# Gated units over batches [0], [1,2], [3,4], [5,6], [7], weights converted in their order of use, exponentials without bias operand, norm of pooled queries

## The chip, the core and the metric

The kernel runs on one core of a Trainium2 chip. The metric is the device time of one execution in microseconds (us). The core's engines run their own instruction queues, each in order: TensorE (PE in the profile; its weight loads are PEld) multiplies matrices, VectorE (DVE), ScalarE (ACT) and GpSimd (POOL) work element by element, and SyncE (SP) issues the DMA transfers.

## The reference, cut to what matters

```python
def _attn_ref(q, k, v):                       # B, H, S, D = 8, 8, 1152, 64
    q_pool = q.reshape(B, H, S // 2, 2, D).mean(axis=3)
    scores = 1 / np.sqrt(D) * np.matmul(q_pool, k.transpose(0, 1, 3, 2))
    scores = scores - np.max(scores, axis=-1, keepdims=True)
    attn = np.exp(scores)
    attn = attn / (np.sum(attn, axis=-1, keepdims=True) + 1e-09)
    return np.matmul(attn, v)                 # 576 rows a head

def _moe_ref(x, w_in, w_spatial, b_spatial, w_out):   # x: 8 x 576 x 512
    h = np.maximum(x @ w_in, 0.0)                     # w_in: 512 x 1024
    u, v = h[..., :512], h[..., 512:]
    v_n = (v - mean(v)) / np.sqrt(var(v) + 1e-06)     # over the last axis
    v_s = np.einsum('ts,bsd->btd', w_spatial, v_n) + b_spatial[None, :, None]
    return (u * v_s) @ w_out                          # w_out: 512 x 512
```

The attention's output, heads side by side, is the second function's x. `w_in` and `w_out` arrive as 64-bit floats.

## The kernel before

Every matrix product is made of products of 16-bit halves: a number is split into a head (ScalarE, `head`) and a rest (VectorE, `rest`), after a scaling by a power of two that is found from the sum of squares (`square_sum` on ScalarE, then `scales`: a matmul with ones and three small VectorE operations).

**Attention** goes over 32 pairs; pair i holds two heads of one batch, four pairs make a batch (`NHP = 4`). While pair i's scores, exponentials and products with v are made (`attention(i)`, 40 steps), generators beside it are stepped at fixed rates (`Pace`): the row maxima of pair i+1 (`maxima`, 27 matmuls, each followed by a VectorE maximum over 384 columns), the loading and splitting of v (`values_ahead`), and the preparation of pair i+2's queries and keys (`prep`). `prep` squares and sums keys and both halves of the queries, then adds the halves (the pooling) on GpSimd. A score tile of 128 x 512 goes through PSUM tile `pss` (three buffers) into an exponential on ScalarE (`main_tile`), with `lnp`, a constant column of log 64, as bias and `esc`, the pair's scale, as scale. GpSimd splits the result (`split`, tile `pt`), and TensorE multiplies it with v into `o`. The maxima go into the scores as two more rows of the contraction, stored in `xq`.

**Gated units.** The second function runs in units of two batches (`gated_unit`), four in all. A unit makes 9 tiles of v (L582), their mean and variance, an inverse square root of 16 small operations on VectorE (L611 to L614), u in 12 pieces (L646) with `normalise` of one v tile after each of the first nine, 8 spatial products with the gate (L688, L689), `split(0)` of the product, and 9 output tiles (L731). While pairs run, the unit in front of the list `units` gets 0.5 of its steps per attention step (`MOE_RATE`); what is left at the end is drained. The last unit splits its product in two groups, so that a spatial product stands between them.

**Weights** are converted on the way: `load_weights` takes `w_in` in 8 pieces and `w_out` in 4, two staging tiles in turn (the next piece's transfer is issued before the present one is used), 0.25 steps per attention step (`W_RATE`), done by the end of pair 7; then `load_spatial` is stepped from within the first unit's v tiles. `from_double` makes a 32-bit float from two integer words.

The program order so written is then rearranged, engine by engine, when the program is built: an instruction can move ahead of others that aren't ready. Each engine keeps the built order on the chip.

Of the kernel before, what the change touches and what calls it, by code (L numbers as in the profile page):

```python
# [13 lines left out]
I32 = mybir.dt.int32  # L14
I64 = mybir.dt.int64
AF = mybir.ActivationFunctionType
# [15 lines left out]
def attn_sgu_kernel(ctx: ExitStack, tc: tile.TileContext, qT, kT, v, w_in, w_spT, b_sp, w_out, out):  # L32
# [18 lines left out]
    NU = B // 2  # L51
    WS_STEPS = 2
    MOE_RATE = 0.5
    D1 = D + 1
    VW = 2 * D + 2

# [18 lines left out]
    lnp = const.tile([P, 1], F32, name="lnp")  # L75
    nc.vector.memset(lnp, math.log(PEXP))
# [67 lines left out]
    def from_double(dst, src, t1, t2):  # L144
# [3 lines left out]
        lo, hi = src[:, 0::2], src[:, 1::2]  # L148
        V.tensor_scalar(out=t1, in0=hi, scalar1=0xFFFFF, scalar2=None, op0=ALU.bitwise_and)
        nc.scalar.activation(dst, t1, AF.Copy, bias=1.0, scale=2.0 ** -20)  # L150
        V.tensor_scalar(out=t2, in0=lo, scalar1=1, scalar2=None, op0=ALU.logical_shift_right)
        yield
        V.scalar_tensor_tensor(out=dst, in0=t2, scalar=2.0 ** -51, in1=dst, op0=ALU.mult, op1=ALU.add)
# [12 lines left out]
    def load_weights():  # L166
        for name, w, wh, wl, n, m in (("wi", w_in, wi_h, wi_l, NCC, DF), ("wo", w_out, wo_h, wo_l, NFC, DM)):
            f32 = mo.tile([P, NT * DH], F32, name="u")
            raw = mo.tile([P, NT * DH], F32, name="vv")

            st = [raw[:, j * 1024 : (j + 1) * 1024].bitcast(I32) for j in range(2)]
            t1, t2 = (raw[:, 2048 + j * 512 : 2560 + j * 512].bitcast(I32) for j in range(2))
            jk = raw[:, 3072 : 3072 + 512]
            pieces = [(c, a) for c in range(n) for a in range(0, m, 512)]
            sq = const.tile([P, len(pieces)], F32, name=name + "q")

            def fetch(j):
                c, a = pieces[j]
                nc.sync.dma_start(out=st[j % 2].bitcast(I64), in_=w[c * P : (c + 1) * P, a : a + 512])

            fetch(0)
            for j, (c, a) in enumerate(pieces):
                if j + 1 < len(pieces):
                    fetch(j + 1)
                d = f32[:, c * m + a : c * m + a + 512]
                yield from from_double(d, st[j % 2], t1, t2)
                square_sum(sq[:, j : j + 1], d, jk)
            s, wsc[name] = yield from scale_of(sq, name)
            yield
            for c, a in pieces:  # L190
                d = f32[:, c * m + a : c * m + a + 512]
                head(wh[:, c, a : a + 512], d, s)
                rest(wl[:, c, a : a + 512], d, s, wh[:, c, a : a + 512])
                yield

    def load_spatial():
        f32 = mo.tile([P, NT * DH], F32, name="u")
        sq = const.tile([P, 5], F32, name="wsq")
        w5 = f32[:, : 5 * S].rearrange("p (c s) -> p c s", s=S)
        nc.sync.dma_start(out=w5[:, 0:4, :], in_=w_spT[0:MAIN, :].rearrange("(c p) s -> p c s", p=P))  # L200
        for half in range(2):
            nc.sync.dma_start(out=w5[half * TAIL : (half + 1) * TAIL, 4, :], in_=w_spT[MAIN:S, :])
        nc.sync.dma_start(out=b_bc, in_=b_sp.rearrange("(o s) -> o s", o=1).broadcast_to([P, S]))
        yield
        for c in range(5):
            square_sum(sq[:, c : c + 1], w5[:, c, :], ws_l[:, c, :])
            yield
        s, wsc["ws"] = yield from scale_of(sq, "ws")
        yield
        for c in range(5):  # L210
            head(ws_h[:, c, :], w5[:, c, :], s)
            rest(ws_l[:, c, :], w5[:, c, :], s, ws_h[:, c, :])
            yield

# [58 lines left out]
    def prep(i):  # L273
# [6 lines left out]

        sq = sm.tile([P, 2], F32, name="sq", bufs=2)
        for j in range(2):
            square_sum(sq[:, j : j + 1], kq[:, j * KEYS : (j + 1) * KEYS], KL[:, 0].rearrange("p c k -> p (c k)"))
            yield
# [5 lines left out]
        st["esc"] = esc  # L290
        s_k, s_q = s[:, 0:1], s[:, 1:2]
        nc.gpsimd.tensor_add(q0, q0, q1)
# [24 lines left out]
    def maxima(i):  # L317
# [34 lines left out]
        nc.vector.reduce_max(out=mx, in_=mt, axis=AX.X)  # L352
        yield
# [23 lines left out]
    W_RATE = 0.25  # L377
    W_AT = 4
    MAX_RATE = 1.0

    units = []

    def unit_step():
        if step(units[0]) is None:
            units.pop(0)
# [3 lines left out]
    def ends_unit(i):  # L389
        return i % (2 * NHP) == 2 * NHP - 1  # L390
# [59 lines left out]
    def turn_main(i):  # L450

        b, hp = divmod(i, NHP)
        n, e = divmod(b, 2)
# [6 lines left out]
        if hp == NHP - 1:  # L460
# [5 lines left out]
            if ends_unit(i):  # L466
                units.append(gated_unit(n))
# [30 lines left out]
    def attention(i):  # L498
# [10 lines left out]
        def main_tile(pt, c, h):  # L509
            ps = ps_s.tile([P, MAIN], F32, name="pss")  # L510
            products(ps, c, h, MAINS[h])
            nc.scalar.activation(pt, ps, AF.Exp, bias=lnp, scale=esc)  # L512

        def tail_tile(h, n):
# [5 lines left out]
            nc.scalar.activation(ptl[:, a:z, h], o, AF.Exp, bias=lnp, scale=esc)  # L520
# [25 lines left out]
    def gated_unit(un):  # L546
        b0, b1 = 2 * un, 2 * un + 1

        tiles = [(j * P, [(b0, j * P, 0, P)]) for j in range(4)]
        tiles.append((MAIN, [(b0, MAIN, 0, TAIL), (b1, MAIN, TAIL, P)]))  # L550
        tiles += [(MAIN + P + j * P, [(b1, j * P, 0, P)]) for j in range(4)]
        pieces = ((0, MAIN), (MAIN, MAIN + P), (MAIN + P, S2))
        last = un == NU - 1
        turn = [0]

        def bank():
# [9 lines left out]
        r_h = sm.tile([P, 3], F32, name="r_h")  # L566
# [269 lines left out]
    for g in units:  # L836
        drain(g)
# [45 lines left out]
```

## Time and profile before

| | |
|---|---|
| median of 3 runs | 1370.36 us (1369.91 to 1372.92) |
| profiled execution | 1378.83 us, span 1377.1 us, mean granted TensorE clock 0.967 |
| busy PE, PEld | 1222.1 us (89%), 741.5 us (54%) |
| busy DVE, ACT, POOL | 967.1 us (70%), 970.6 us (70%), 847.0 us (62%) |
| DMA | 123.77 MB, mean 90 GB/s |
| first exponential starts, last one | 48.5 us, 1265.7 us |

A share of busy time is a mean over stages with different limits. A busy TensorE isn't TensorE at its peak, since matmuls overlap; how many it starts in a stretch tells more. The granted clock is the share of full speed that TensorE got.

### The profile page before, as it was taken

Reading aid. Unit: us, or ns where it says so; the run is one execution under the profiler, and the core shown is the slowest. Engines: PE = TensorE matmul, PEld = TensorE weight load, DVE = VectorE, ACT = ScalarE, POOL = GpSimd, SP = SyncE. Lnnn points to the kernel's source line nnn. Section 1 sums busy time; section 2 is a strip of 40 time slices with the busy share of each in tenths; the row PEclk is TensorE's granted clock in tenths of the full one; section 3 lists DMA queues with packets and bytes.
Section 4 is the critical chain, followed back from the end, with each engine's and each line's share of the span. In section 5 each row is a group of like instructions: output and inputs, shape, how many; then the busy total and the mean of one; then the engine's idle time right before and its main releaser. Section 6 shows DMA issues by size and latency. Waiting matters only on the chain.

```text
span 1377.1 us, 33478 instructions
## 1 busy us (share of the span) xinstructions
PE 1222.1 (89%) x13696; PEld 741.5 (54%) x13696; DVE 967.1 (70%) x2068; ACT 970.6 (70%) x1632; POOL 847.0 (62%) x492
## 2 busy tenths in 40 slices
PE   3677887788998999889998999889998999899998
PEld 1354555555554665556555666555555566556443
DVE  5799889986869767765668766775667866761455
ACT  6777678779966777768776886768776776655333
POOL 3587677878755666657774766667666576655000
PEclk9998899989999999999999999999999999999999
DMA  7533343434333231244332132244331131101002
GB/s 252 166 97 109 94 124 94 128 93 139 113 96 96 79 94 56 62 126 135 96 96 87 51 91 84 74 118 135 104 96 42 47 94 55 28 24 40 8 1 69
DMA packets 56346, 123.77 MB, mean 90 GB/s; under 512 B 8256, under 2 KB 16448, under 8 KB 56192
## 3 DMA queue, kind: packets, MB, share of 16 engines
q1 hardware_dynamic: 56192, 121.63, 29.8%
q8 instruction: 107, 1.75, 0.5%
q14 instruction: 47, 0.39, 0.1%
HBM read 83.56 MB, written 9.44 MB: 68 GB/s over the span
## 4 chain that ended last, share of the span: by engine, by line
PE 47%; DVE 25%; ACT 8%; POOL 7%; DMA 7%; issue 4%; SPq 1%; POOLq 0%; ACTq 0%; DVEq 0%
DVE mt L348 7%; PE pss L507 5%; PE pss L506 5%; PE pw L688 5%; POOL pt L524 4%; PE pm L342 4%; PE pw L731 4%; PE pw L646 3%; PE o L435 3%; PE o L428 3%; PE pw L582 3%; ACT pt L512 3%; DMA kq<-in_qT_dram 3%; PE o L432 3%; DVE vv L138 2%
## 5 line engine op out<-in xcount | busy, mean ns | idle before, releaser
L524 POOL TENSOR_TENSOR pt<-pt 128x1024 f16<-128x1024 f32 x288 | 567.8, 1977 | 265.9 <-ACT pt L512 253.8
L512 ACT ACTIVATE pt<-pss,lnp,esc 128x512 f32<-128x512 f32 x576 | 439.4, 776 | 156.7 <-PE pss L507 148.1
L348 DVE TENSOR_REDUCE mt<-pm 128x1 f32<-128x384 f32 x730 | 395.8, 552 | 139.1 <-PE pm L342 119.2
L435 PE MATMUL o<-vp,pt 128*128 128x65 f16 x2304 | 282.8, 198 | 20.2 <-POOL pt L524 19.9
L428 PE MATMUL o<-vp,pt 128*128 128x65 f16 x2304 | 284.8, 196 | 13.0 <-DVE xm L443 12.8
L506 PE MATMUL pss<-qhi,khi 128*128 128x64 f16 (+1 forms) x1152 | 279.6, 294 | 9.1 <-ACT pt L512 8.0
L432 PE MATMUL o<-vp,pt 128*128 128x64 f16 x2304 | 284.5, 196 | 0.0
L507 PE MATMUL pss<-xq,klo 66*128 66x64 f16 (+1 forms) x1152 | 280.6, 295 | 4.1 <-DMA xq<-mr 4.1
L428 PEld LDWEIGHTS <-pt 128*128 128x128 bf16 x2304 | 222.7, 101 | 85.1 <-DVE xm L443 22.0
L432 PEld LDWEIGHTS <-pt 128*128 128x128 bf16 x2304 | 221.6, 100 | 50.7 <-issue 10.5
L342 PE MATMUL pm<-khi,qhi 128*128 128x384 f16 x652 | 217.9, 335 | 32.6 <-DVE mt L348 27.7
L435 PEld LDWEIGHTS <-pt 128*128 128x128 f16 x2304 | 220.7, 100 | 31.6 <-POOL pt L524 24.8
L507 PEld LDWEIGHTS <-klo 66*128 66x128 f16 x1152 | 99.1, 100 | 48.8 <-issue 17.3
L132 ACT ACTIVATE klo<-kq 128x1152 f16<-128x1152 f32 x64 | 74.6, 1166 | 63.7 <-DMA kq<-in_kT_dram 49.4
L506 PEld LDWEIGHTS <-khi 128*128 128x128 f16 x1152 | 103.5, 100 | 27.9 <-issue 12.2
L342 PEld LDWEIGHTS <-qhi 128*128 128x128 f16 x768 | 76.8, 101 | 66.3 <-issue 28.5
L524 POOL TENSOR_TENSOR ptl<-ptl 128x1152 f16<-128x1152 f32 x32 | 71.1, 2221 | 57.9 <-ACT ptl L520 57.9
L305 POOL TENSOR_TENSOR klo<-kq,khi 128x640 f16<-128x640 f32 x64 | 85.1, 1341 | 20.1 <-ACT khi L304 19.8
L520 ACT ACTIVATE ptl<-pss,lnp,esc 128x256 f32<-128x256 f32 (+1 forms) x128 | 75.6, 591 | 24.8 <-PE pss L507 24.2
L264 POOL TENSOR_TENSOR vp<-vt,vp 128x576 f16<-128x576 f32 x64 | 80.6, 1264 | 20.3 <-ACT vp L262 20.3
L582 PE MATMUL pw<-wi_h,xg 128*128 128x512 f16 x240 | 90.1, 382 | 0.0
L731 PE MATMUL pw<-wo_h,vv 128*128 128x512 f16 x216 | 80.3, 381 | 4.7 <-DVE vv L138 4.7
(177 smaller groups left out, 2394.2 us busy)
## 6 DMA issues: line engine op xcount, KB each, us to landing
vt<-in_v_dram SPq DMA_DIRECT2D x64, 576.0 KB
kq<-in_kT_dram SPq DMA_DIRECT2D x32, 576.0 KB
kq<-in_qT_dram SPq DMA_DIRECT2D x32, 576.0 KB
khi<-khi SPq DMA_DIRECT2D x96, 144.0 KB
out_dram<-row SPq DMA_DIRECT2D x24, 256.0 KB
qhi<-xq SPq DMA_DIRECT2D x64, 72.0 KB
klo<-klo SPq DMA_DIRECT2D x32, 144.0 KB
vv<-in_w_in_dram SPq DMA_DIRECT2D x8, 512.0 KB
```

The source lines that it names most:

```text
L305: nc.gpsimd.tensor_sub(KL[:, 0, a:z], k0[:, a:z], khh[:, 1, a:z])
L342: nc.tensor.matmul(pm[:, :W], lhsT=qhl[:, h, c0 : c0 + P], rhs=khh[:, h, n * NB : (n + 1) * NB, :], start=True, stop=True,)
L348: nc.vector.reduce_max(out=mt[:, t, n : n + 1], in_=pm[:, :W], axis=AX.X)
L428: nc.tensor.matmul(o[:, t], lhsT=top[:, cols], rhs=vp[:, D : D + D1], start=c == 0 and t == 0, stop=False, skip_group_check=True,)
L432: nc.tensor.matmul(o[:, t, 0:D], lhsT=top[:, cols], rhs=vp[:, 0:D], start=False, stop=False, skip_group_check=True)
L435: nc.tensor.matmul(o[:, t], lhsT=rst[:, cols], rhs=vp[:, D : D + D1], start=False, stop=c == NC - 1, skip_group_check=True,)
L506: nc.tensor.matmul(o, lhsT=khh[:, h, c, :], rhs=qhl[:, h, q], start=True, stop=False)
L507: nc.tensor.matmul(o, lhsT=KL[0:KR, h, c, :], rhs=X[0:KR, h, q], start=False, stop=True)
L512: nc.scalar.activation(pt, ps, AF.Exp, bias=lnp, scale=esc)
L524: nc.gpsimd.tensor_sub(t.bitcast(F16)[:, :, 0::2], t, t.bitcast(BF16)[:, :, 1::2])
L582: nc.tensor.matmul(ph, lhsT=xa[:, cc, c0 : c0 + P], rhs=wa[:, cc, DH:DF], start=n == 0, stop=n == 3 * NCC - 1,)
L731: nc.tensor.matmul(py, lhsT=ga[:, fc, c0 : c0 + P], rhs=wa[:, fc, :], start=m == 0, stop=m == end - 1)
```

## The change

1. Units are now batch 0 alone, then [1,2], [3,4], [5,6], then batch 7 alone: five instead of four. The first can start after four pairs instead of eight, and gets 0.36 steps per attention step; the others get 0.55. A unit of one batch has 5 tiles instead of 9 (its last tile holds 64 rows that are already in another) and makes u in 8 pieces of 288 columns.
2. Weights are converted in the order in which a unit needs them: the half of `w_in` for v, the half for u, the spatial weights, `w_out`, at 0.34 steps per attention step. There is one staging tile; the next piece's transfer is issued when the present one has been used. `need` steps the conversion to the end of a part if a unit comes early. Unit 0's tiles `u0` and `vv0` share their memory with the conversion.
3. `from_double` no longer shifts the low word: it is read as unsigned, with a stride of two words.
4. The exponentials have no bias operand. Instead `prep` makes a column `lnp` from the pair's scales (a VectorE operation and a minimum), and `maxima` subtracts it from the row maxima.
5. `prep` adds the query halves first, on GpSimd, and ScalarE squares the 576 columns of the sum instead of 1152.
6. Any unit that runs after the last score may use the score buffers `pss` (before: the last unit). Only the last unit, batch 7, has two groups.

```diff
-    NU = B // 2
-    WS_STEPS = 2
-    MOE_RATE = 0.5
+    UNITS = [(0,)] + [(b, b + 1) for b in range(1, B - 1, 2)] + [(B - 1,)]
+    NU = len(UNITS)
+    MOE_RATE = [0.36] + [0.55] * (NU - 1)
+    W_RATE = 0.34
+    W_AT = 4
...
-        lo, hi = src[:, 0::2], src[:, 1::2]
+        lo, hi = src.bitcast(U32)[:, 0::2], src[:, 1::2]
         V.tensor_scalar(out=t1, in0=hi, scalar1=0xFFFFF, scalar2=None, op0=ALU.bitwise_and)
         nc.scalar.activation(dst, t1, AF.Copy, bias=1.0, scale=2.0 ** -20)
-        V.tensor_scalar(out=t2, in0=lo, scalar1=1, scalar2=None, op0=ALU.logical_shift_right)
         yield
-        V.scalar_tensor_tensor(out=dst, in0=t2, scalar=2.0 ** -51, in1=dst, op0=ALU.mult, op1=ALU.add)
+        V.scalar_tensor_tensor(out=dst, in0=lo, scalar=2.0 ** -52, in1=dst, op0=ALU.mult, op1=ALU.add)
...
+    def load_matrix(name, w, wh, wl, a, x0):
+        st = vv0[:, V_FREE : V_FREE + 1024].bitcast(I32)
...
+        fetch(0)
+        yield
+        for c in range(n):
+            d = u0[:, x0 + c * 512 : x0 + (c + 1) * 512]
+            yield from from_double(d, st, t1, t2)
+            if c + 1 < n:
+                fetch(c + 1)
+            square_sum(sq[:, c : c + 1], d, t1.bitcast(F32))
+            yield
...
+        yield from load_matrix("wiv", w_in, wi_h, wi_l, DH, 0)
+        ready.add("wiv")
+        yield from load_matrix("wiu", w_in, wi_h, wi_l, 0, U_FREE)
+        ready.add("wiu")
+        yield from load_spatial()
+        ready.add("ws")
+        yield from load_matrix("wo", w_out, wo_h, wo_l, 0, U_FREE)
+        ready.add("wo")
+    weights = Pace(load_weights(), W_RATE, W_AT)
+    def need(name):
+        while name not in ready:
+            weights.gen = step(weights.gen)
...
+        nc.gpsimd.tensor_add(q0, q0, q1)
         sq = sm.tile([P, 2], F32, name="sq", bufs=2)
-        for j in range(2):
-            square_sum(sq[:, j : j + 1], kq[:, j * KEYS : (j + 1) * KEYS], KL[:, 0].rearrange("p c k -> p (c k)"))
-            yield
+        square_sum(sq[:, 0:1], kq[:, 0:KEYS], junk)
+        yield
+        yield
+        square_sum(sq[:, 1:2], q0, junk[:, :S])
+        yield
...
+        nc.vector.scalar_tensor_tensor(
+            out=lnp, in0=s[:, 0:1], scalar=math.log(PEXP) / ESC, in1=s[:, 1:2], op0=ALU.mult, op1=ALU.mult
+        )
+        nc.vector.tensor_scalar_min(lnp, lnp, 2.0 ** 29)
-        nc.gpsimd.tensor_add(q0, q0, q1)
...
         nc.vector.reduce_max(out=mx, in_=mt, axis=AX.X)
+        nc.vector.tensor_scalar_sub(mx, mx, st["lnp"])
...
-            nc.scalar.activation(pt, ps, AF.Exp, bias=lnp, scale=esc)
+            nc.scalar.activation(pt, ps, AF.Exp, bias=0.0, scale=esc)
...
-            if last and turn[0] % 5 > 1:
+            if not scores_left[0] and turn[0] % 5 > 1:
                 return ps_s.tile([P, MAIN], F32, name="pss")
...
+            weights.tick()
+            if units:
+                credit = min(credit + MOE_RATE[units[0][0]], 2.0)
```

Three places in the built order. First VectorE, where the conversion meets the scales of a prepared pair; before, in pair 3:

```order
L348 TENSOR_REDUCE mt<-pw 128x1 x2
L151 TENSOR_SCALAR vv<-vv 128x512
L117 TENSOR_SCALAR qkh<-pm 128x2
L153 SCALAR_TENSOR_TENSOR u<-vv,u 128x512
L348 TENSOR_REDUCE mt<-pm 128x1
L121 TENSOR_SCALAR qks<-qkh 128x2
L402 TENSOR_TENSOR xg<-pm,xg 128x512
L122 TENSOR_SCALAR qkr<-qkh 128x2
L348 TENSOR_REDUCE mt<-pm 128x1
L287 SCALAR_TENSOR_TENSOR esc<-qkr 128x1
```

and now, in pair 1 (line 413 is the maximum, 346 `esc`, 171 the conversion's first operation):

```order
L139 TENSOR_SCALAR qkh<-pm 128x2
L171 TENSOR_SCALAR vv<-vv 128x512
L413 TENSOR_REDUCE mt<-pm 128x1
L143 TENSOR_SCALAR qks<-qkh 128x2
L144 TENSOR_SCALAR qkr<-qkh 128x2
L413 TENSOR_REDUCE mt<-pw 128x1
L346 SCALAR_TENSOR_TENSOR esc<-qkr 128x1
L352 SCALAR_TENSOR_TENSOR lnp<-qks 128x1
L413 TENSOR_REDUCE mt<-pm 128x1
L355 TENSOR_SCALAR lnp<-lnp 128x1
```

The shift (151) is gone, and two operations for `lnp` stand behind `esc`.

Second, VectorE where unit 0 is normalised: before in pair 10, with the conversion of `w_in` and `w_out` over:

```order
L618 TENSOR_SCALAR row<-vv,mv,rs 128x512
L348 TENSOR_REDUCE mt<-pm 128x1
L618 TENSOR_SCALAR row<-vv,mv,rs 128x512
L402 TENSOR_TENSOR xg<-pm,xg 128x512
L624 TENSOR_TENSOR vv<-row,vv 128x512 x2
L348 TENSOR_REDUCE mt<-pm 128x1 x5
```

and now in pair 6 (703 and 709 normalise, 171 and 174 convert):

```order
L703 TENSOR_SCALAR row<-vv,mv,rs 128x512
L413 TENSOR_REDUCE mt<-pm 128x1 x2
L709 TENSOR_TENSOR vv<-row,vv 128x512
L413 TENSOR_REDUCE mt<-pm 128x1 x3
L703 TENSOR_SCALAR row<-vv,mv,rs 128x512
L171 TENSOR_SCALAR vv<-vv 128x512
L413 TENSOR_REDUCE mt<-pm 128x1 x2
L709 TENSOR_TENSOR vv<-row,vv 128x512
```

Normalising and conversion now share VectorE with the maxima.

Third, TensorE after the last score, at the matmul with ones that begins the split of a unit's product; before, in the last unit:

```order
L688 MATMUL pw<-ws_l,vv 128x512
L689 LDWEIGHTS vv
L689 MATMUL pw<-ws_l,vv 128x64
L112 MATMUL pm<-gt,ones 128x1
L688 LDWEIGHTS vv
L688 MATMUL pss<-ws_h,vv 128x512
L689 LDWEIGHTS vv
L689 MATMUL pss<-ws_h,vv 128x64
```

and now, in unit [5,6] (775 and 776 are the spatial product, 820 the output):

```order
L775 MATMUL pw<-ws_l,vv 128x512
L776 LDWEIGHTS vv
L776 MATMUL pss<-ws_l,vv 128x64
L134 MATMUL pm<-gt,ones 128x1
L820 LDWEIGHTS vv
L820 MATMUL pss<-wo_h,vv 128x512
L820 LDWEIGHTS vv
L820 MATMUL pss<-wo_l,vv 128x512
```

Where a further spatial product followed the matmul with ones, the outputs follow it now.

More of the change, by code (lines that the diff above doesn't have):

```diff
@@ L164, in attn_sgu_kernel @@
     wsc = {}
[L166 to L188, printed above, removed]
-            yield
[L190 to L193, printed above, removed]
-                yield
@@ L519, in tail_tile @@
             o = ps[:, : (z - a) * TAIL].rearrange("p (c s) -> p c s", s=TAIL)
-            nc.scalar.activation(ptl[:, a:z, h], o, AF.Exp, bias=lnp, scale=esc)
+            nc.scalar.activation(ptl[:, a:z, h], o, AF.Exp, bias=0.0, scale=esc)
         def split(t):
@@ L662, in gated_unit @@
                 yield
+        need("ws")
+        r_v = sm.tile([P, 1], F32, name="r_v")
+        nc.vector.tensor_scalar_mul(r_v, wsc["ws"], 1.0 / SVN)
         groups = [(0, 2), (2, NFC)] if last else [(0, NFC)]
@@ L743, in gated_unit @@
         if not last:
-            for e in range(2):
+            for e in range(nb):
                 for fc in range(NFC):
@@ L754, in gated_unit @@
         else:
-            order = [(e, fc) for fc in range(NFC) for e in range(2)]
-            ahead = 2 * groups[0][1] + 1
+            order = [(e, fc) for fc in range(NFC) for e in range(nb)]
+            ahead = nb * groups[0][1] + 1
             for e, fc in order[:ahead]:
@@ L764, in gated_unit @@
             next(second)
[L765 removed]
+            for t in range(nt):
                 py = yield from products(0, t)
```

197 lines of the change are left out of this document (117 added, 80 removed).

## The prediction

> **What bounds the kernel now.** I read the page first, then the busy times by stretch, then the stretches that fall out of line, then groups and waits. Page, the slices and the chain that ended last:
>
> ```profile
> PE   3677887788998999889998999889998999899998
> DVE  5799889986869767765668766775667866761455
> PEclk9998899989999999999999999999999999999999
> PE 47%; DVE 25%; ACT 8%; POOL 7%; DMA 7%; issue 4%; SPq 1%; POOLq 0%; ACTq 0%; DVEq 0%
> DVE mt L348 7%; PE pss L507 5%; PE pss L506 5%; PE pw L688 5%; POOL pt L524 4%; PE pm L342 4%; PE pw L731 4%; PE pw L646 3%; PE o L435 3%; PE o L428 3%; PE pw L582 3%; ACT pt L512 3%; DMA kq<-in_qT_dram 3%; PE o L432 3%; DVE vv L138 2%
> ```
>
> TensorE carries the end, VectorE takes over in places, ScalarE little. Which where? I cut the span at the first exponential of pairs 0, 4, 8, 12 and 31 (a pair is two heads of one batch, four pairs a batch) and at the last exponential:
>
> ```profile
> 0.00:48.50 48.50, 16.31 (x51) 5.90 (x52) 27.96 (x65) 30.95 (x62) 17.12 (x22) 1.00 0.71 226
> 48.50:189.20 140.70, 113.05 (x1397) 73.74 (x1397) 123.38 (x224) 104.57 (x176) 105.64 (x58) 0.90 0.40 116
> 189.20:328.60 139.40, 111.53 (x1409) 73.63 (x1408) 123.12 (x235) 111.13 (x188) 108.91 (x60) 0.89 0.35 103
> 328.60:490.00 161.40, 148.56 (x1655) 90.40 (x1654) 115.10 (x259) 128.51 (x222) 105.85 (x63) 0.96 0.35 105
> 490.00:1236.70 746.70, 697.28 (x8158) 427.73 (x8155) 520.95 (x1154) 538.76 (x890) 489.00 (x281) 0.99 0.28 82
> 1236.70:1266.50 29.80, 29.80 (x376) 18.71 (x375) 3.11 (x11) 18.90 (x28) 18.59 (x10) 1.00 0.14 46
> 1266.50:1377.10 110.60, 105.53 (x667) 51.34 (x663) 53.53 (x123) 37.83 (x71) 1.90 (x1) 1.00 0.08 27
> ```
>
> (Columns: stretch, length, busy PE, weight loads, DVE, ACT, POOL, granted clock, DMA.) Pairs 0 to 7 go by VectorE: 123 of 140 us. From pair 8 on TensorE holds: 697 of 747. After the last exponential a whole gated unit runs alone, 110.6 us. Inside the TensorE stretch some pairs stand out:
>
> ```profile
> 405.00:451.30 46.30, 40.27 (x432) 24.26 (x430) 41.49 (x89) 31.95 (x55) 25.91 (x15) 0.93 0.25 74
> 568.60:609.50 40.90, 33.23 (x383) 20.26 (x382) 32.02 (x60) 28.49 (x47) 22.55 (x13) 1.00 0.29 79
> 722.30:768.70 46.40, 40.69 (x432) 24.23 (x430) 41.14 (x89) 31.73 (x55) 25.07 (x14) 0.93 0.24 72
> 768.70:806.20 37.50, 36.54 (x440) 23.10 (x439) 22.69 (x55) 30.82 (x53) 27.91 (x18) 1.00 0.31 89
> ```
>
> Pairs 10 and 18 normalise a unit's v: 46 us with VectorE at 41, against 37.5 in the next pair. Pair 14 splits a unit's product: 40.9 us, while TensorE has the least to do.
>
> **The change, part by part.** Durations are of the profiled execution, 1378.83 us with a span of 1377.1; the runs shown have a median of 1370.36. I work out a difference and add it to the median.
>
> Streams of matmuls are costed by the spacing of their starts:
>
> ```profile
> 1350.34 0.59 PE L731 MATMUL pss<-wo_h,xg 128*128 128x512 f16 x2
> 1350.77 0.38 PE L731 MATMUL pss<-wo_l,xg 128*128 128x512 f16 x1
> 300.01 0.19 PE L507 MATMUL pss<-xq,klo 66*128 66x64 f16 x1
> 300.04 0.19 PE L506 MATMUL pss<-qhi,khi 128*128 128x64 f16 x1
> ```
>
> Two 512-wide in 0.43: 0.216 us each; 64-wide 0.03; in proportion 288-wide 0.122 and 128-wide 0.056 (estimates from these). With the counts of the instruction order, gated work is, before and after: pairs 4 to 7, 0 and 24.7 us; 8 to 11, 48 and 27; 12 to 30, 229 and 233. In all some 5 us is added, since a unit of one batch puts 64 rows into a 128-row tile. So TensorE's work is moved, hardly changed; the question is what it meets where it lands.
>
> *Vector work in pairs 0 to 11.*
>
> ```profile
> L151 DVE TENSOR_SCALAR vv<-vv 128x512 int32<-128x512 int32 x9 | 12.9, 1438 | 0.1
> L287 DVE SCALAR_TENSOR_TENSOR esc<-qkr 128x1 f32<-128x1 f32 x8 | 10.6, 1329 | 0.0
> L287 DVE SCALAR_TENSOR_TENSOR esc<-qkr x32: 142/160/1952, 9.0 to 1171.1; 128x1 f32<-128x1 f32 x32
> L592 DVE BATCH_NORM_STATS2 stt<-vv 128x6 f32<-128x512 f32 x27 | 18.6, 689 | 31.9 <-ACT vv L590 31.9
> L618 DVE TENSOR_SCALAR row<-vv,mv,rs 128x512 f32<-128x512 f32 x27 | 28.1, 1049 | 0.3
> L624 DVE TENSOR_TENSOR vv<-row,vv 128x512 f16<-128x512 f32 x27 | 29.4, 1113 | 0.5 <-ACT vv L623 0.4
> L613 DVE TENSOR_SCALAR sd<-sd 128x9 f32<-128x9 f32 x12 | 6.8, 566 | 0.2
> L524 POOL TENSOR_TENSOR pt<-pt 128x1024 f16<-128x1024 f32 x288 | 567.8, 1977 | 265.9 <-ACT pt L512 253.8
> ```
>
> The shift of line 151 goes: 12 times up to 1.44, 14 us in all over some nine pairs. The strided read of `lo` moves into the next operation; unseen, I price it between nothing and what 151 lost, and take nothing, since that operation streams as many elements as before. Added per pair: `lnp` (two tiny operations) and a subtraction on nine columns. The first is of `esc`'s kind: between 0.14 and 1.95 us; I take 1.3 in pairs 0 to 7, the row's mean there, and 0.3 for the other two. Here the Trainium skill, "SBUF — State Buffer", section "Who interferes with whom", speaks against the change: a vector operation with two SBUF inputs waits for a whole GpSimd operation, since one lock covers both. That agrees with 142 against 1952 ns, GpSimd's split being 1977; by the rule at its worst each new operation costs 1.98, and the sum is 5 us more for the eight pairs.
>
> Pairs 0 to 3: four shifts less (-5.8), 4 x 1.6 more (+6.4), and by the order some 5 us of conversion now falls later: -4. Price range -8 to +3.
>
> Pairs 4 to 7: unit 0 adds 5 x 0.69 statistics, 16 small operations (about 0.35 each, between `esc`'s 0.16 and L613's 0.57: 5.6) and 5 x (1.05 + 1.11) normalising: 20 us; the later conversions about 5; less six shifts (8.6) plus 4 x 1.6: +23. At the stretch's own 139.4 of wall for 123.1 of VectorE that would be +26; pair 10 holds the same mixture at 46.3/41.5, so +25. I take **+22**, as pairs 0 to 7 still have ScalarE and TensorE idle beside it. Ends: 0 (it fits in the gaps) and +30.
>
> Pairs 8 to 11: TensorE loses 21 us of stream and VectorE the normalising of a double unit: 161.4 goes towards four times 34: **-24**. Ends -18 and -32.
>
> *Pairs 12 to 30.* TensorE +4. At 0.55 steps for 0.5 the unit is 10% denser and pauses for 0.7 pair between units; three normalising pairs (14, 22, 30) and two splits, where there were two and three. Each such pair exceeds its neighbour by 9 us (46.4 to 37.5); 10% denser on a VectorE of 41 is 1.5 to 2 each. **+9**; ends 0 and +15.
>
> *The end.* After the last score the order leaves 6.6 spatial products, the split and nine output tiles of unit 3, then all of unit 4: 97.5 us of stream against 101 before. But unit 3's split is one group, with nothing of TensorE between its last spatial product and its outputs, and before the last unit had two groups with a product between them. The hole, by vector and scalar rows of the tail:
>
> ```profile
> L138 DVE SCALAR_TENSOR_TENSOR xg<-u,gs,xg 128x576 f16<-128x576 f32 x8 | 6.3, 817 | 2.2 <-ACT xg L135 2.2
> L135 ACT ACTIVATE xg<-u,gs 128x576 f16<-128x576 f32 x8 | 5.8, 764 | 2.6 <-DVE gs L121 2.6
> L695 DVE SCALAR_TENSOR_TENSOR row<-pw,r_v,b_bc 128x512 f32<-128x512 f32 x24 | 18.0, 750 | 19.3 <-PE pw L689 18.8
> L132 ACT ACTIVATE vt<-vt 128x576 f32<-128x576 f32 x64 | 43.2, 677 | 0.3 <-DMA vt<-in_v_dram 0.3
> ```
>
> bias and product about 2, square 0.7, scale chain about 1, then seven of eight splits at 0.8, of which first outputs hide half: 7 to 8 us. **+5**; ends 0 and +10.
>
> *Scalar work.*
>
> ```profile
> L512 ACT ACTIVATE pt<-pss,lnp,esc 128x512 f32<-128x512 f32 x576 | 439.4, 776 | 156.7 <-PE pss L507 148.1 <-PE o L435 3.9 <-POOL pt L524 1.5
> L590 ACT ACTIVATE vv<-pw,r_h 128x512 f32<-128x512 f32 x30 | 20.5, 684 | 6.3 <-PE pw L582 6.0
> L132 ACT ACTIVATE klo<-kq 128x1152 f16<-128x1152 f32 x64 | 74.6, 1166 | 63.7 <-DMA kq<-in_kT_dram 49.4 <-DMA kq<-in_qT_dram 8.8 <-DMA khi<-khi 5.5
> POOL kq L292 <- ACT klo L132: 55.6, 12, 13.0
> ```
>
> An exponential with one pointer less costs, by the row with only a scale, 684 for 776: 576 + 128 times 0.092 is 65 us of ScalarE, 2 a pair; the pooled square saves 0.49 a pair (677 for 1166). What hides it is ScalarE waiting 148 us for the scores. On the chain `pt` has 3%, 41 us, of which 12% is 5; ends 0 and -10, I take **-4**. The pooling add no longer waits for both squares but for the transfer; it stands in GpSimd's queue ahead of the splits as before: 0, within 2 us. The start: the square of the queries now stands behind four squares of v, some 6 us later, but all v scales are done earlier: **+1**, between -4 and +4.
>
> Sum: -4 + 22 - 24 + 9 + 5 - 4 + 1 = **+5**, that is 1375.4 of the median; I say 1375, own range 1366 to 1386.
>
> **The rivals.** *Faster: the moved work is free.* TensorE in pairs 4 to 7 has 28 of 139 us idle; if VectorE's 123 is mostly waiting on GpSimd, unit 0 rides there: +22 becomes +3, the sum -14, 1356. For it: the granted clock of 0.89 there; a fuller TensorE could hold 1.00. Against: 88% VectorE, and pair 10. It decides if pairs 4 to 7 stay below 150 us. The Trainium skill, "TensorE: Matmul & The Clock Gate", Part 1, says an idle window halves the clock, which favours this rival; the 0.89 agrees.
>
> *Same: the terms cancel.* ScalarE's cut is worth 8 rather than 4, through the splits that wait for it: 1371.
>
> *Much slower: one staging tile.* Weights were fetched one piece ahead; now the next fetch follows the last use, behind `kq` on SP's queue, and VectorE stands in order before it, with the maxima queued behind.
>
> ```profile
>   DVE vv L149: 1.5, 1
> 20.93 6.80 DMA vt<-in_v_dram
> 35.01 4.02 DMA vt<-in_v_dram
> ```
>
> Before it waited once. Transfers of like size took 4.0 to 6.8; if 2 of that shows in each of 12 pieces: +24, 1399. Against: the order puts each conversion well behind its fetch.
>
> **How the numbers follow.** Forecast 0.45 (0.37 above +0.2%, 0.08 within, that being about what a measurement here can tell), free ride 0.32, cancelling 0.11 (0.09 within), one staging tile 0.12. Faster 0.34, same 0.17, slower 0.49. The range leaves out less than 2 in 10: 1349, a little under the free ride, to 1398.
>
> **What would show it.** Pairs 4 to 7 near 161 us with VectorE at 145, pairs 8 to 11 near 137; pairs 14, 22, 30 of 47 to 49; a TensorE hole of 7 us after unit 3's last spatial product; exponentials of 0.685; the shift's row gone and `lnp` at 0.3 to 1.3. Wrong if VectorE waits for weight transfers, or if pairs 4 to 7 stay at 140.

## The result and the profile after

The changed kernel takes 1465.05 us (median of 4 runs, 1459.82 to 1473.97), against 1371.64 for the kernel before on the same chip: ratio 1.0686, 95% interval 1.0630 to 1.0742. The forecast was 1375 with a range up to 1398: slower was right, the size was not. The profiled execution took 1473.97 us, the longest of the four, with a span of 1472.2. One execution of all the runs below, of a_noQ_oldU at a granted clock of 0.66, took 1742 us and is left out. The changed kernel's page, the busy times, two engines by slices and the chain that ended last:

```profile
PE 1245.4 (85%) x13772; PEld 757.7 (51%) x13772; DVE 1009.0 (69%) x2192; ACT 907.8 (62%) x1635; POOL 841.8 (57%) x492
PE   3677778778888889798989889888988989889898
DVE  5798887988775666967684656765867555772525
PE 39%; DVE 28%; POOL 11%; ACT 9%; DMA 7%; issue 5%; SPq 1%; POOLq 0%; DVEq 0%; ACTq 0%
```

TensorE is busy 23 us more in a span that is 95 us longer. On the chain its share falls from 47% to 39%, while GpSimd's rises from 7% to 11%. The stretches, cut as before (start; pairs 0 to 3, 4 to 7, 8 to 11, 12 to 30; pair 31; after the last exponential; columns as before):

```profile
0.00:45.30 45.30, 13.54 (x51) 5.83 (x52) 23.59 (x62) 27.36 (x56) 15.00 (x21) 0.86 0.66 215
45.30:187.60 142.30, 111.38 (x1412) 73.13 (x1412) 126.41 (x239) 101.67 (x187) 110.00 (x61) 0.91 0.40 120
187.60:354.40 166.80, 133.55 (x1533) 86.99 (x1533) 140.71 (x290) 118.75 (x220) 105.20 (x60) 0.90 0.35 105
354.40:504.10 149.70, 128.35 (x1609) 81.09 (x1606) 107.33 (x238) 100.02 (x179) 103.94 (x61) 0.99 0.33 97
504.10:1323.90 819.80, 720.62 (x8074) 436.32 (x8073) 552.91 (x1228) 505.19 (x898) 487.35 (x282) 0.97 0.26 75
1323.90:1355.90 32.00, 32.00 (x425) 20.64 (x423) 6.46 (x16) 18.10 (x32) 18.46 (x10) 1.00 0.01 2
1355.90:1472.20 116.30, 106.00 (x683) 53.68 (x679) 51.59 (x123) 36.67 (x69) 1.90 (x1) 0.97 0.09 31
```

| stretch | before | after | difference | forecast |
|---|---|---|---|---|
| start | 48.5 | 45.3 | -3.2 | +1 |
| pairs 0 to 3 | 140.7 | 142.3 | +1.6 | -4 |
| pairs 4 to 7 | 139.4 | 166.8 | +27.4 | +22 |
| pairs 8 to 11 | 161.4 | 149.7 | -11.7 | -24 |
| **pairs 12 to 30** | 746.7 | 819.8 | **+73.1** | **+9** |
| pair 31 and the end | 140.4 | 148.3 | +7.9 | +5 |

(The forecast's -4 for shorter exponentials belongs to no single stretch.)

Three quarters of the loss lie in pairs 12 to 30, where TensorE's instructions are even 84 fewer and its idle time is 99 us instead of 49. That idle time is 50 of the 73; the other 23 are longer busy time, at a granted clock of 0.97 instead of 0.99. Who waits for whom? Rows of the view of waits (engine, what it waited for, us in total, times, longest), each over the whole span: three of the kernel before, then the same three of the changed kernel with a new one, and groups of the new and shortened operations:

```profile
POOL pt L524 <- ACT pt L512: 253.8, 132, 5.5
PE pm L342 <- DVE mt L348: 27.7, 35, 2.2
POOL klo L305 <- ACT khi L304: 19.8, 13, 2.9
```
```profile
POOL pt L590 <- ACT pt L578: 377.8, 173, 7.4
PE pm L407 <- DVE mt L413: 72.7, 71, 4.2
ACT klo L154 <- POOL kq L336: 50.8, 24, 3.5
POOL klo L370 <- ACT khi L369: 50.4, 27, 9.5
L578 ACT ACTIVATE pt<-pss,esc 128x512 f32<-128x512 f32 x576 | 385.0, 682 | 186.4 <-PE pss L573 168.8
L418 DVE TENSOR_SCALAR mx<-mx,lnp 128x9 f32<-128x9 f32 x32 | 30.6, 957 | 0.7
L352 DVE SCALAR_TENSOR_TENSOR lnp<-qks 128x1 f32<-128x1 f32 x32 | 19.1, 597 | 0.0
L355 DVE TENSOR_SCALAR lnp<-lnp 128x1 f32<-128x1 f32 x32 | 4.7, 146 | 0.0
```

The wait of ScalarE for GpSimd is new: the square of the pooled queries (L154) stands in ScalarE's queue until GpSimd has added them (L336), with the exponentials behind it. That was the first suspect, called theory Q; X is the small vector operations for `lnp`, U the new units and their rates.

### The profile page after: what moved, and what is told of

Same layout as the page of the kernel before. It is cut to its first block, busy times and chain, and to the rows that moved or that the text cites. A ratio compares the mean times of both kernels' runs of the same rounds, so it can differ in the third digit from the quotient of the medians.

```text
span 1472.2 us, 33654 instructions
## 1 busy us (share of the span) xinstructions
PE 1245.4 (85%) x13772; PEld 757.7 (51%) x13772; DVE 1009.0 (69%) x2192; ACT 907.8 (62%) x1635; POOL 841.8 (57%) x492
## 4 chain that ended last, share of the span: by engine, by line
PE 39%; DVE 28%; POOL 11%; ACT 9%; DMA 7%; issue 5%; SPq 1%; POOLq 0%; DVEq 0%; ACTq 0%
DVE mt L413 8%; POOL pt L590 6%; PE pss L573 4%; PE pss L572 4%; PE pm L407 4%; PE pw L730 3%; PE pw L667 3%; ACT pt L578 3%; PE pw L775 3%; DMA kq<-in_kT_dram 3%; DMA vt<-in_v_dram 3%; PE pw L820 3%; PE o L501 2%; PE o L494 2%; POOL kq L336 2%
## 5 line engine op out<-in xcount | busy, mean ns | idle before, releaser
L590 POOL TENSOR_TENSOR pt<-pt 128x1024 f16<-128x1024 f32 x288 | 557.0, 1938 | 390.5 <-ACT pt L578 377.8
L413 DVE TENSOR_REDUCE mt<-pm 128x1 f32<-128x384 f32 x757 | 408.7, 551 | 179.0 <-PE pm L407 156.5
L578 ACT ACTIVATE pt<-pss,esc 128x512 f32<-128x512 f32 x576 | 385.0, 682 | 186.4 <-PE pss L573 168.8
L494 PE MATMUL o<-vp,pt 128*128 128x65 f16 x2304 | 286.2, 197 | 11.8 <-DVE xm L509 11.7
L572 PE MATMUL pss<-qhi,khi 128*128 128x64 f16 (+1 forms) x1152 | 281.1, 294 | 12.4 <-ACT pt L578 12.0
L407 PE MATMUL pm<-khi,qhi 128*128 128x384 f16 x673 | 224.0, 336 | 78.7 <-DVE mt L413 72.7
L494 PEld LDWEIGHTS <-pt 128*128 128x128 bf16 x2304 | 225.7, 102 | 102.6 <-issue 40.7
L498 PEld LDWEIGHTS <-pt 128*128 128x128 bf16 x2304 | 223.7, 101 | 49.0 <-issue 11.9
L154 ACT ACTIVATE klo<-kq 128x1152 f16<-128x1152 f32 x64 | 58.9, 921 | 85.5 <-POOL kq L336 50.8
L667 PE MATMUL pw<-wi_h,xg 128*128 128x512 f16 x272 | 103.8, 386 | 0.0
L320 POOL TENSOR_TENSOR vp<-vt,vp 128x576 f16<-128x576 f32 x64 | 84.1, 1315 | 27.3 <-ACT vp L318 27.3
L730 PE MATMUL pw<-xg,wi_h 128*128 128x512 f16 (+2 forms) x376 | 88.2, 326 | 0.0
L586 ACT ACTIVATE ptl<-pss,esc 128x256 f32<-128x256 f32 (+1 forms) x128 | 63.9, 499 | 27.0 <-PE pss L573 25.7
```

The source lines that it names most:

```text
L407: nc.tensor.matmul(pm[:, :W], lhsT=qhl[:, h, c0 : c0 + P], rhs=khh[:, h, n * NB : (n + 1) * NB, :], start=True, stop=True,)
L413: nc.vector.reduce_max(out=mt[:, t, n : n + 1], in_=pm[:, :W], axis=AX.X)
L494: nc.tensor.matmul(o[:, t], lhsT=top[:, cols], rhs=vp[:, D : D + D1], start=c == 0 and t == 0, stop=False, skip_group_check=True,)
L498: nc.tensor.matmul(o[:, t, 0:D], lhsT=top[:, cols], rhs=vp[:, 0:D], start=False, stop=False, skip_group_check=True)
L572: nc.tensor.matmul(o, lhsT=khh[:, h, c, :], rhs=qhl[:, h, q], start=True, stop=False)
L578: nc.scalar.activation(pt, ps, AF.Exp, bias=0.0, scale=esc)
```

## The experiments

Each run is compared with runs of the kernel before on the same chip (medians of 1370.7 to 1374.0 us). Stretches are those of one profiled execution each; that of the kernel before, 1378.8 us, lies some 8 us above its median, so differences of a few us between stretches tell little. Names that begin with a_ start from the changed kernel, with b_ from the one before.

**1. Parts undone, and done alone.** Four runs: the pooled norm undone; the exponentials' bias operand back; the old units and rate; and, from the kernel before, pooled norm and exponentials without bias together.

```diff
 a_noQ, in prep (a_noX: the bias operand back, lnp and its subtraction out)
-        nc.gpsimd.tensor_add(q0, q0, q1)
-        square_sum(keys); yield; yield; square_sum(q0); yield
+        square_sum(keys); yield; square_sum(both halves); yield
 ...
+        nc.gpsimd.tensor_add(q0, q0, q1)      # after the scales
 a_oldU (and unit 0 gets tiles of its own)
-    UNITS = [(0,)] + [(b, b + 1) for b in range(1, B - 1, 2)] + [(B - 1,)]
+    UNITS = [(b, b + 1) for b in range(0, B, 2)]
-    MOE_RATE = [0.36] + [0.55] * (NU - 1)
+    MOE_RATE = [0.5] * NU
```

> The changed kernel with one part undone: the two raw halves are squared first and the queries are pooled after the scales, as before. Theory Q (ScalarE, which goes in order, now stands at the square of the pooled queries until GpSimd has added them, 50.8 us in all, and the exponentials and splits behind it come late): most of the 94 us come back, 1385 to 1405. Theory X (the two lnp operations and the subtraction on VectorE hold up the maxima): 1455 to 1470, as all of it is still there. Theory U (the units of other size and their rates): also 1455 to 1470.

Measured 1429.07 us, ratio 1.0409 (1.0380 to 1.0439): 36 of 93 us come back. That is in no range: the pooled norm holds a good third of the loss.

> The changed kernel with the exponentials' bias operand back and without lnp and its subtraction. Theory X: the maxima no longer wait behind the small vector operations, 1385 to 1410, although every exponential is 0.09 us longer. Theory Q: 1455 to 1475. Theory U: 1460 to 1480, since only the longer exponentials show.

1462.95, ratio 1.0660 (1.0625 to 1.0694): nothing comes back as long as the pooled norm is there.

> The changed kernel with the gated units over batches [0,1], [2,3], [4,5], [6,7] and 0.5 steps as before; weights, exponentials and pooled norm stay changed. Theory U (the new cut of the units and 0.55 steps cost the time in pairs 12 to 30): 1370 to 1390. Theories Q and X: the pairs from 12 on lose as much as in the changed kernel, some 70 us, so 1430 to 1450.

1445.27, ratio 1.0530 (1.0503 to 1.0557): the units hold 20.

> The kernel before with the pooled norm and the exponentials without bias operand alone; old units, old weights, shift kept. Theories Q and X (either or both cost the 73 us of pairs 12 to 30): 1425 to 1450. Theory U: 1360 to 1375, as the exponentials are shorter and nothing else is dear.

1438.27, ratio 1.0473 (1.0444 to 1.0502). So 64 of the loss arise without any change to units and weights. Theory U falls as the main cause.

**2. Each alone, and both undone.**

> The kernel before with the pooled norm alone. Theory Q alone (ScalarE stands at the square of the pooled queries for GpSimd's add): the 64 us that both edits cost together in the kernel before are all here, 1425 to 1445. Theory X alone: 1370 to 1380. Both needed, each for half: about 1405.

1442.03, ratio 1.0507 (1.0483 to 1.0530): the pooled norm alone costs 69 us, the largest part.

> The kernel before with the exponentials without bias operand alone (lnp per pair, subtracted from the maxima). Theory Q: faster or the same, 1360 to 1375. Theory X: 1420 to 1445. Half and half: about 1405.

1393.45, ratio 1.0139 (1.0098 to 1.0181): above theory Q's 1375 and below half and half's 1405; `lnp` and its exponentials cost 20 by themselves.

> The changed kernel with both the pooled norm and the exponentials without bias undone: left are the units, the weights and the shift. Theory Q with U: 1395 to 1430, the 1429 of the kernel without the pooled norm alone, or a little below it. If the lnp operations cost anything once the pooled norm is gone: 1385 to 1405. If units and weights cost nothing: 1365 to 1375.

1398.98, ratio 1.0201 (1.0166 to 1.0237): units, weights and shift cost 26 together. The forecast's terms for this part, without `lnp` and exponentials, add up to -4, so it missed here too, by 30. And `lnp` with its exponentials costs 30 (1429 to 1399) once the pooled norm is gone, against 2 while it is there (a_noX): the two don't add.

> The changed kernel with the old norm of queries and the old units and rate: left are the weights in their order of use, the missing shift and the exponentials without bias. If pooled norm and units together hold the whole loss: 1360 to 1380. If the lnp operations or the weights' single staging tile cost as well: 1390 to 1415.

1418.60 (the middle one of three executions), ratio 1.0319 (1.0270 to 1.0368). The second expectation, or more: with old units the weights, shift and exponentials still cost 46. That isn't the pooled norm or the units; it stays open below.

**3. Why does the pooled norm cost?** It saves ScalarE 16 us of squares (by the page's rows 74.6 before, 58.9 after) and adds a wait and one more empty step in `prep` (two `yield`s in place of one). The diff of the change shows the step, but neither its list nor the prediction speaks of it. It got a run of its own:

```diff
 b_yield, in prep, after the two squares
             square_sum(sq[:, j : j + 1], ...)
             yield
+        yield
 b_Q_dve, against b_Q: the pooling add on VectorE, a step later
-        nc.gpsimd.tensor_add(q0, q0, q1)
         square_sum(keys); yield
-        yield
+        nc.vector.tensor_add(q0, q0, q1)
+        yield
         square_sum(q0)
 ...
 a_noQ_nosub: a_noQ with exponentials of bias 0.0 and without lnp and the subtraction
 b_S, in from_double
-        V.tensor_scalar(out=t2, in0=lo, scalar1=1, scalar2=None, op0=ALU.logical_shift_right)
 ...                                        # the low word read as unsigned, as in the change
```

> The kernel before with one empty step more in the preparation of each pair, after the two squares: no instruction is added, what follows comes one step (some three score tiles) later. Theory Q1: 1370 to 1380. Theory Q2: 1410 to 1445.

1415.40, ratio 1.0313 (1.0288 to 1.0337). An empty step costs 43 us: not one instruction is added.

> The kernel before with the pooled norm, the pooling add on VectorE one step after the square of the keys instead of on GpSimd with it. Theory Q1 (ScalarE, in order, waits for an add that stands behind splits in GpSimd's queue): the wait is gone, 1365 to 1385. Theory Q2 (the extra step in the preparation shifts all that follows it, whoever adds): as with GpSimd, 1425 to 1445. Theory Q3 (the square of the pooled queries must wait for both transfers, whoever adds): 1405 to 1430.

1402.47, ratio 1.0225 (1.0200 to 1.0249): in no range, and below the empty step alone. A step more, without the wait and with GpSimd relieved of the add, costs 30. So with the step in place, moving the add off GpSimd brings back 39 of b_Q's 69 us: theory Q1 isn't refuted by the price of the step.

> The changed kernel with the old norm of queries and exponentials without bias operand, but without lnp and its subtraction: the factor of 64 on the exponentials is left out. Theory X1 (the three small vector operations a pair hold the maxima and cost the 30 us between 1399 and 1429): 1390 to 1402. Theory X2 (the shorter exponentials change the order of the built program for the worse): 1420 to 1435.

1413.30, ratio 1.0304 (1.0276 to 1.0331): in neither range, half each. Of the 30 us of `lnp`, 16 go with its three operations; 14 stay with exponentials that are merely shorter. Why these cost time was not found.

> The kernel before with the shift of the weights' low words gone (12 vector operations of 1.44 us in pairs 0 to 9). If VectorE bounds those pairs: 1362 to 1369. If it costs or brings nothing: 1370 to 1376.

1368.11, ratio 0.9974 (0.9960 to 0.9987): a small gain, as expected if VectorE bounds. In which pairs it lies isn't shown: in the profiled executions pairs 0 to 3 take 132.6 us for 140.7, but 134.6 in b_yield too, which keeps the shift.

**4. The step or the wait?** The pooled norm with one step between the squares, in the kernel before and in the changed one (one `yield` taken out, nothing else):

> The kernel before with the pooled norm, but one step between the two squares as before, so that the preparation has no step more. ScalarE has less time between GpSimd's add and the square that needs it. If the extra step is the larger part (the empty step alone cost 43): 1390 to 1415. If ScalarE's wait for GpSimd is the larger part: 1420 to 1450.

1393.26, ratio 1.0163 (1.0126 to 1.0200). With the empty step this makes a square: neither 1373, step 1415, pooled norm without step 1393, both 1442. The step costs 43 or 49, the pooled norm itself 22 or 27. ScalarE's wait for GpSimd in pairs 12 to 30 of both kernels (first b_Q, then b_Q_1y), and that stretch:

```profile
ACT klo L132 <- POOL kq L281: 26.9, 14, 3.8
505.51:1299.93 794.42, 712.57 (x8155) 435.31 (x8152) 545.64 (x1154) 532.88 (x890) 486.42 (x281) 0.97 0.27 77
```
```profile
ACT klo L132 <- POOL kq L281: 21.1, 14, 2.8
499.60:1249.58 749.98, 698.43 (x8158) 429.53 (x8156) 520.52 (x1154) 531.17 (x890) 488.82 (x281) 0.99 0.28 81
```

ScalarE waits for GpSimd 14 times in both, for 26.9 and 21.1 us; but without the step the stretch takes 750.0 us, 3 more than before, and with it 794.4. So the wait that looked like the culprit costs this stretch next to nothing without the step. Together with it, it costs more: b_yield takes 782.2 here, b_Q 12 more, and b_Q_dve, with the step but without the wait for GpSimd, 778.5. What the pooled norm costs without the step lies in pairs 0 to 11 (13.3 us of the profiled execution). There b_Q_dve is 20.6 us shorter than b_Q, so the wait, or GpSimd's add itself, is a likely cause; it was not followed further.

> The changed kernel with one of the two empty steps ahead of the square of the pooled queries taken out, so that the preparation has as many steps as before; pooled norm and ScalarE's wait for GpSimd stay. Theory of the step (its place costs, as in the kernel before, where taking it out brought 1442 to 1393): 1410 to 1430. Theory of the wait (ScalarE stands for GpSimd's add): 1450 to 1470.

1433.49 (1425.43 to 1443.64), ratio 1.0443 (1.0402 to 1.0484), a little above the range for the step and well below that for the wait. In the changed kernel, too, the step holds 32 of the 36 us that undoing the pooled norm brought, by the medians. Its pairs 12 to 30, and those of a_noQ:

```profile
504.04:1276.20 772.16, 702.25 (x8065) 428.20 (x8064) 543.75 (x1227) 505.32 (x896) 487.90 (x281) 0.98 0.27 79
```
```profile
510.54:1279.19 768.65, 703.85 (x8065) 429.32 (x8064) 538.18 (x1227) 512.74 (x896) 486.41 (x281) 0.98 0.27 79
```

Of the 73 us lost in this stretch (819.8 against 746.7) one empty step holds 47.6 in these two profiled executions. That is more than its share of the medians, since 1473.97 is the longest of four and a_Q1y's 1425.43 the shortest of four.

**5. Why does an empty step cost?** The tile `kq`, one pair's keys and queries, has one buffer. Load, squares, scales, head, splits of the keys, next load: that is a loop, once a pair. The tile's instructions in the kernel before and in b_yield, over one such loop (shortest, median and longest in ns, then first and last start in us; b_yield's own load went out at 677.2, ahead of its rows):

```profile
L222 SPq DMA_DIRECT2D kq<-in_kT_dram x2: 577/730/883, 666.3 to 704.8; - x2
L132 ACT ACTIVATE klo<-kq x4: 1163/1164/1164, 671.9 to 713.1; 128x1152 f16<-128x1152 f32 x4
L135 ACT ACTIVATE xq<-kq,qks x1: 762/762/762, 697.9 to 697.9; 128x576 f16<-128x576 f32 x1
L304 ACT ACTIVATE khi<-kq x2: 616/670/725, 700.7 to 701.3; 128x640 f16<-128x640 f32 x1, 128x512 f16<-128x512 f32 x1
```
```profile
L132 ACT ACTIVATE klo<-kq x4: 1162/1163/1164, 682.4 to 725.0; 128x1152 f16<-128x1152 f32 x4
L135 ACT ACTIVATE xq<-kq,qks x1: 759/759/759, 707.6 to 707.6; 128x576 f16<-128x576 f32 x1
L305 ACT ACTIVATE khi<-kq x2: 624/676/728, 711.5 to 712.8; 128x640 f16<-128x640 f32 x1, 128x512 f16<-128x512 f32 x1
L222 SPq DMA_DIRECT2D kq<-in_kT_dram x1: 597/597/597, 716.2 to 716.2; - x1
```

Before, a load is issued at 666.3, its keys are squared at 671.9, the head is made at 697.9, the next load goes out at 704.8: 38.5 us, a pair's length. One loop tells little, since the way from squares to head differs from pair to pair (2.4 to 33.6 us before). The means over the loads of pairs 10 to 30, worked out from these instructions' times in each trace. The ways to the square and to the head end where these start, the others where the named instruction ends; in the kernel before and in b_yield GpSimd's pooling add falls into the way to the head:

| us | load to square | two squares | to the head | head to last copy | last subtraction | to next load | loop |
|---|---|---|---|---|---|---|---|
| before | 4.8 | 5.0 | 18.4 | 6.8 | 2.7 | 1.2 | 38.8 |
| b_yield | 5.1 | 4.8 | 21.2 | 6.2 | 2.1 | 1.4 | 40.9 |
| b_Q_1y | 4.6 | 6.1 | 17.9 | 6.6 | 2.6 | 1.3 | 39.1 |
| b_Q | 5.2 | 6.4 | 20.4 | 6.2 | 2.1 | 1.4 | 41.7 |
| after | 5.5 | 5.8 | 19.8 | 6.1 | 2.7 | 1.7 | 41.7 |

The step lengthens the way from squares to head by 2.9 us (2.5 from b_Q_1y to b_Q), the loop by 2.2 (2.7). A table can't tell whether the loop sets the pair's length or follows it. A second buffer can: the keys' half gets two, the queries keep one.

```diff
-        kq = ld.tile([P, 2 * KEYS], F32, name="kq")
+        kt = ld.tile([P, KEYS], F32, name="kt", bufs=2)
+        qt = ld.tile([P, KEYS], F32, name="qt")
```

> The kernel before with the keys' load buffer doubled (the queries' stays single), so that the next keys are fetched while the last are still being split. Theory L (a loop through the one buffer, load to squares to scales to splits to next load, fills a whole pair and sets its length): the squares no longer wait for the keys' transfer, 1350 to 1368. Theory O (the built order only happens to be good or bad): 1368 to 1385, no gain.

1360.30, ratio 0.9922 (0.9894 to 0.9950): faster, by 10 us, as theory L expected.

> The kernel before with the pooled norm and the doubled key buffer. Theory L: the loop has slack for the extra step and the wait, so most of the 69 us come back, 1370 to 1395. Theory O: 1425 to 1445, as without the buffer.

1408.58, ratio 1.0285 (1.0236 to 1.0333): between the two ranges: 33 of 69 come back, and 36 don't.

> The changed kernel whole, with the doubled key buffer. Theory L: the loss by pooled norm and subtraction is mostly gone, 1395 to 1420 (25 us of units, weights and shift and some 15 of lnp remain). Theory O: 1450 to 1470.

1443.81, ratio 1.0538 (1.0498 to 1.0577): again between the ranges: 21 come back. Theory L holds for a fifth to a half of the loss, not for all of it. The chain of b_k2 (TensorE carries 59% where it carried 47%), the squares' waits for the keys' transfer in the kernel before and in b_k2, and then pairs 12 to 30 of b_k2 and b_Q_k2:

```profile
PE 59%; DVE 24%; ACT 5%; POOL 5%; DMA 3%; issue 3%; SPq 0%; POOLq 0%; DVEq 0%; ACTq 0%
```
```profile
ACT klo L132 <- DMA kq<-in_kT_dram: 49.4, 20, 4.7
```
```profile
ACT klo L132 <- DMA kt<-in_kT_dram: 2.6, 1, 2.6
475.90:1217.95 742.05, 699.82 (x8158) 430.80 (x8157) 517.72 (x1154) 541.56 (x889) 488.59 (x280) 0.98 0.28 81
```
```profile
493.77:1265.65 771.88, 704.84 (x8158) 431.67 (x8157) 542.00 (x1154) 532.46 (x891) 484.21 (x281) 0.98 0.27 78
```

The last row shows what the buffer can't mend. VectorE runs the same 1154 instructions in 542.0 us, where b_k2 takes 517.7 and b_Q_1y 520.5; b_yield and b_Q take 542 and 546. Of the kernels with these instructions, those with the extra step have the slower vector operations. Which? The pair's scale `esc` and the gate's product in the TensorE stretch (the shortest, median and longest in ns), of the kernel before, then of b_yield and b_Q_k2:

```profile
L287 DVE SCALAR_TENSOR_TENSOR esc<-qkr x18: 143/160/1014, 501.3 to 1171.1; 128x1 f32<-128x1 f32 x18
L698 DVE TENSOR_TENSOR u<-u,row x48: 215/682/1941, 495.5 to 1197.2; 128x512 f32<-128x512 f32 x24, 128x64 f32<-128x64 f32 x24
```
```profile
L288 DVE SCALAR_TENSOR_TENSOR esc<-qkr x18: 140/160/1740, 511.0 to 1214.1; 128x1 f32<-128x1 f32 x18
L699 DVE TENSOR_TENSOR u<-u,row x48: 207/748/2387, 497.3 to 1235.1; 128x512 f32<-128x512 f32 x24, 128x64 f32<-128x64 f32 x24
```
```profile
L292 DVE SCALAR_TENSOR_TENSOR esc<-qkr x18: 136/872/1740, 513.0 to 1206.8; 128x1 f32<-128x1 f32 x18
```

An operation of 0.15 us takes up to 1.74. The 18 of `esc` are busy for 4.5 us in the kernel before, for 15.1 in b_yield: half of VectorE's difference of 21. The timeline shows how, VectorE and then GpSimd, first of b_yield, then of the changed kernel:

```profile
628.74 1.74 DVE L288 SCALAR_TENSOR_TENSOR esc<-qkr 128x1 f32<-128x1 f32 x1
628.57 1.90 POOL L525 TENSOR_TENSOR pt<-pt 128x1024 f16<-128x1024 f32 x1
```
```profile
707.03 1.90 DVE L785 TENSOR_TENSOR u<-u,row 128x64 f32<-128x64 f32 x1
706.96 1.90 POOL L590 TENSOR_TENSOR pt<-pt 128x1024 f16<-128x1024 f32 x1
```

`esc` starts under a split and ends with it, and so does a product of 64 columns. In b_yield's stretch 8 of the 18 `esc` start under a split; each of them takes 1.58 to 1.74 us and ends with it, and the other ten take 0.14 to 0.16. The Trainium skill, "SBUF — State Buffer", section "Who interferes with whom", says that a vector operation with two SBUF inputs waits for a whole GpSimd operation; these rows agree. So a step that only shifts where the small operations fall can put them under splits, and the maxima, for which TensorE waits, stand behind them. That wait in the stretch, in the kernel before and in b_yield:

```profile
PE pm L342 <- DVE mt L348: 15.6, 18, 2.2
```
```profile
PE pm L343 <- DVE mt L349: 30.0, 37, 2.2
```

Without the step it is 14.1 to 15.7 us (b_k2, before, b_Q_1y), with it 26.6 to 30.3 (b_Q, b_yield, b_Q_k2). That the operations and this wait got longer is shown; that they make up the rest of the step's price is argued from their size (21 to 25 us of VectorE and 11 to 16 of the wait, against 25 of the stretch in b_Q_k2), since no run moved them alone.

**6. A version that beats both.**

> The kernel before with two things the runs spoke for: the shift of the weights' low words gone (alone 1368) and the keys' load buffer doubled (alone 1360). If they add: 1353 to 1359. If both draw on the same idle time of pairs 0 to 7: 1358 to 1364.

1366.14, ratio 0.9939 (0.9915 to 0.9963). That is above both ranges: the two gains don't add. Why isn't shown: pairs 0 to 3 take 132.6 us (shift gone), 131.2 (buffer) and 130.9 (both) in the profiled executions, but the execution of the kernel before, 140.7 there, was a long one. Both versions are faster than the kernel before. The lowest median is that of two key buffers alone, 1360.3, but its interval (0.9894 to 0.9950) overlaps that of both together, so which of the two is faster isn't shown.

## Why the prediction was wrong

Undone one after the other, the parts hold (forecast in brackets): the pooled norm 36 us (0), `lnp`'s three operations 16 (13), the shorter exponentials 14 (-4), units, weights and shift 26 (-4). That "slower" came out right was largely luck: the +5 was what terms of both signs left over, and three of these four parts were mis-sized.

- **The failed step** is the one on scalar work: "The pooling add no longer waits for both squares but for the transfer ...: 0, within 2 us." I priced the operations and the wait, not the place of the steps behind them, although the diff shows the second `yield`. The pooled norm costs 69 us in the kernel before and 36 in the changed one; of that the extra empty `yield` is 43 to 49, and 32. The add on GpSimd, with the wait for it, was mis-sized too: with the step in place, adding on VectorE brings back 39.
- **"Pairs 12 to 30: +9; ends 0 and +15."** Measured +73.1. In the profiled executions undoing the pooled norm takes 51.1 of it (819.8 to 768.7), undoing `lnp` 4.2 more (to 764.5); units, weights and shift keep +17.8, just past the upper end. The denser unit with its three normalising pairs (50.1, 49.4 and 50.7 us, foreseen 47 to 49) was the right mechanism, too small.
- **`lnp`**, priced at 1.6 us in each of pairs 0 to 7, some 13: undoing it brings 15.6 there (profiled a_noQ and a_noQX); undoing the three operations alone (a_noQ_nosub) brings 12.4. The sum was right, its parts by luck: the three take 0.36, 0.14 and 1.23 us in these pairs, 1.7 together, where 1.3 and 0.3 were foreseen. The prediction's worst case, 1.98 for each new operation, comes to 35 us more over the eight pairs; its 5 counts the first operation alone. The shorter exponentials, forecast -4, gained nothing that shows: without `lnp`'s operations they still cost 14, and why stays open.
- **Pairs 4 to 7, +22, and 8 to 11, -24.** Measured +27.4 and -11.7, and +21.7 and -13.9 with pooled norm and `lnp` undone (first row below; the second is pairs 12 to 30 of the same run). The +22 holds 6.4 for `lnp`, so +21.7 stands against 15.6: right in mechanism, too small by 6. At 161.1 us it decides against the free ride, which needed under 150. The second was too large by 10.

```profile
180.91:342.05 161.14, 135.14 (x1567) 87.99 (x1566) 141.81 (x282) 128.99 (x225) 107.03 (x61) 0.92 0.37 113
489.55:1254.01 764.46, 699.63 (x8069) 427.09 (x8068) 526.10 (x1172) 549.32 (x896) 483.36 (x282) 0.99 0.27 80
```

- **The end, +5**: +5.7, in part by the mechanism foreseen. TensorE's idle time before its rows after unit 3's last spatial product:

```profile
1387.11 0.35 PE L134 MATMUL pm<-gt,ones 128*128 128x1 f32 x2 [3.41 <-DVE gt L149]
1388.77 0.61 PE L820 MATMUL pss<-wo_h,vv 128*128 128x512 f16 x1 [1.31 <-ACT vv L157]
```

4.7 us of hole, 7 to 8 foreseen. What the forecast didn't have: the output matmuls behind the hole start 0.43 us apart until 1394.3, where 0.22 was reckoned; for these 13 that is some 2.7 us, so part of the agreement is luck.
- **One staging tile**: VectorE waits for weight transfers 9.0 us in all, two times; +24 needed twelve. **Exponentials of 0.685**: 0.682.
- **Open**: the weights were never undone by themselves. With old units and norm, weights, shift and exponentials cost 46 us, the exponentials alone 20 and the shift -4. The rest, near 30, lies for the most part in pairs without any conversion (12 to 30: +27 in that kernel, against +3 in the profiled execution of the exponentials alone, at 1383.5 the fastest of its four), so it isn't the conversion's work. Another shift of the unit's steps against the pair's is one explanation, and not tested.

## What to carry to other kernels

Where generators are stepped at fixed rates, an empty step is an edit like any other: price what it delays, above all a loop through a single-buffered tile whose round trip is as long as an iteration. Look for such loops (load to last use to next load) before a change, and give the tile a second buffer where there is room. The length of a new wait in the list isn't yet its cost: change one thing at a time, as here, where the wait stayed and most of the time went with the step.

## What was not expected of the hardware

VectorE's time for the same 1154 instructions in pairs 12 to 30 varied between 518 and 546 us from kernel to kernel. Half of the difference between the kernel before and b_yield is `esc`, 0.15 us by itself, which took up to 1.74 where it started under a GpSimd split and ended with it.
